# Attention and two MLPs on one core: a 4 KB descriptor ring, a seventh fp32 work tile, and one shared pool of six staging tiles

## The chip, the cores and the metric

The program runs on one core of one Trainium2 chip. The metric is the device time of one execution in microseconds (us). The engines are called PE (TensorE; PEld is its weight load), DVE (VectorE), ACT (ScalarE), POOL (GpSimd) and SP (SyncE, which here only issues DMAs). POOL issues DMAs too.

## The reference

Three stages follow each other. Each is two matrix products with something elementwise between them.

```python
scores = z @ z.T / S                 # B=2, S=3008, d_qk=64
x = u * (relu(scores) ** 2 @ v)      # d_model=256
h = x @ w_in                         # 6016 tokens, d_ff=2048
g = (a0 + a1*h + a2*h**2 + a3*h**3) / (1 + |b0|*|h| + |b1|*h**2 + 1e-6)
x = g @ w_out
h = x @ w2_in
out = (max(h, 0) + alpha * min(h, 0)) @ w2_out
```

The scores of one batch are symmetric, so a block above the diagonal is the transpose of one below it.

## The kernel before, in words

Products are kept near fp32 accuracy by splitting every operand into a high and a low part (`split`: ACT or DVE copies the high part, DVE subtracts at L121), so each product is three matmuls. Attention (`a_stream`) runs over blocks (b, j) of 512 query columns, six to a batch, and in a block over 12 steps kp of 256 key rows. A step makes two score tiles on PE (L393, L394), takes relu and square on ACT (L397, L400) into an fp32 tile `r`, splits it into `ahi` and `alo`, and three steps later (`LAG_A`) multiplies them with the values (L437, L446): 16 matmuls in all. The first MLP (`m1_hidden`, `m1_back`) is woven in between from step 36 of attention on, and weights are decoded, split and spilled to DRAM by POOL's DMAs meanwhile. The second MLP (`m2_*`) comes after attention, with the rest of the first.

For batch 1 (`FOLD`) the symmetry is used. In block j, every step whose key rows belong to a later block is also turned: `turn_block` lets SP issue two DMA transposes (L333) that read `r` as 16-bit words and write the staging tile `xt`, and `save_turned` stores `xt` to DRAM (`rt`, two DMAs at L341), one turn later. In the later block, `load_turned` brings the words back into a staging tile `xd` (two DMAs at L351), and `a_turned` joins them to fp32 (`rr`: ACT copies at L362, DVE at L363) in place of score matmuls. There are 30 turned steps, so 60 transposes, 60 stores and 60 loads.

All fp32 work tiles of 4 KB per partition (`r`, `rr`, `sq`, `ab`, `t`, `dec`, `m`) come from one tag `"t"` with TT = 6 buffers. An `r` that is turned holds its buffer until both its transposes have landed. `xt` has two buffers of its own (XT), and `xd` two (XD). Each engine and each DMA queue works strictly in order. The order on each is made by a scheduler when the program is built, which also chooses the buffer of each tile; a tile waits until the one before it in its buffer has been read for the last time. POOL's DMAs keep their descriptors in a ring at the start of SBUF, 16 KB per partition unless it is set otherwise.

Of the kernel before, what the change touches and what calls it, by code (L numbers as in the profile page):

```python
# [11 lines left out]
U16 = mybir.dt.uint16  # L12
# [3 lines left out]
DRAM = bass.MemoryType.DRAM  # L16


BIG, HL, TT, RAW, ZP, XP = 24, 7, 6, 2, 8, 4

XT, XD, AHEAD = 2, 2, 1

FOLD = ((1, 0),)

# [28 lines left out]
def relu2_attention_rational_mlp_prelu_mlp(  # L53
# [15 lines left out]
    nc = tc.nc  # L69
    P = 128  # L70
# [6 lines left out]
    QB = 512  # L77
# [18 lines left out]
    zctx = ExitStack()  # L96
    zp = zctx.enter_context(tc.tile_pool(name="zp", bufs=ZP))
    wr = zctx.enter_context(tc.tile_pool(name="wr", bufs=WR))
    xdp = zctx.enter_context(tc.tile_pool(name="xdp", bufs=XD))
    late = {}  # L100

    def raw_tile(nm, early=False):
# [173 lines left out]
    xd = {}  # L276
# [46 lines left out]
    def turn_block(b, j, kp, r):  # L323

        kb, k0 = kp // 2, kp % 2 * 2 * P
        if (b, j, kb) not in turned:
            turned[b, j, kb] = dr.tile([2, QB, QB], U16, name=f"rt{b}_{j}_{kb}")
        x = xdp.tile([P, 8, 2 * P], U16, tag="xt", name="xt", bufs=XT)
        ru = r.bitcast(U16)
        w = 0  # L330
        for i in range(2):
            rows = min(P, S - (2 * kp + i) * P)
            nc.sync.dma_start_transpose(out=x[:, :, w : w + rows], in_=ru[0:rows, i, :])  # L333
            w += rows
        unsaved.append((turned[b, j, kb], k0, w, x))
# [10 lines left out]
    def load_turned(b, j, kp):  # L346
        n = qn[j]
        q0 = kp % 2 * 2 * P
        d = xdp.tile([P, 2, 2, QB], U16, tag="xd", name="xd", bufs=XD)
        for h in range(2):  # L350
            nc.sync.dma_start(  # L351
                out=d[:, h, :, :n],
                in_=turned[b, kp // 2, j][h, q0 : q0 + 2 * P, :n].rearrange("(c p) k -> p c k", p=P),
            )
        halves[b, j, kp] = d
# [13 lines left out]
    def a_scores(b, j, kp):  # L369
# [43 lines left out]
        if folded(b, j, kp // 2):  # L413
            turn_block(b, j, kp, r)
# [255 lines left out]
    def a_stream():  # L670
# [4 lines left out]
        def fetch(b, j, kp):  # L675
            while coming and len(halves) < AHEAD + folded(b, kp // 2, j) and (
                coming[0][:2] == (b, j) or coming[0][:2] == (b, j + 1) and kp >= NKP - 2
            ):
                load_turned(*coming.pop(0))
# [190 lines left out]
```

## Time and profile before

| what | value |
|---|---|
| median of 3 runs | 1600.2 us (1598.0 to 1601.96) |
| the profiled execution: its own time | 1600.62 us |
| its span, first to last instruction | 1598.7 us |
| PE busy | 1539.4 us, 96% of the span |
| DVE, ACT, POOL busy | 1413.9, 1172.8, 90.5 us |
| mean granted clock of PE | 0.987 of full speed |

The page cuts the span in 40 slices of 40 us, with the busy tenths of each engine and the granted clock. All is full from slice 20 on, when attention has ended. Slices 9 to 19 are batch 1 of attention, where steps are turned and loaded back, and there PE and its clock show lower digits:

```profile
PE   9999999998989889888999999999999999999999
DVE  8989989896979788999999998999989899998864
PEclk9999999998999899999999999999999999999999
DMA  6364132569897878676700010100001000001000
```

PE and DVE are in tenths of a slice busy, PEclk in tenths of full clock, DMA the mean share of 16 DMA engines.

### The profile page before, as it was taken

How to read it: one execution, taken by the hardware profiler on the slowest of the kernel's cores; microseconds unless marked ns; L12 is line 12 of the kernel's file. 1: busy time of each engine (PE TensorE's matmuls, PEld its weight loads, DVE VectorE, ACT ScalarE, POOL GpSimd, SP SyncE). 2: the span in 40 equal slices, each digit the busy share in tenths (PEclk: the TensorE clock that was granted, in tenths of full speed). 3: DMA queues.
4: the chain of work that ended last, by engine and by line, in shares of the span. 5: the costliest groups of instructions: out<-in, count | busy, mean ns of one | idle time of the engine just before them, and what ended most of it. 6: DMA issues, size and time to landing. Idle time of an engine off the chain costs nothing.

```text
span 1598.7 us, 18271 instructions
## 1 busy us (share of the span) xinstructions
PE 1539.4 (96%) x6776; PEld 1271.4 (80%) x6776; DVE 1413.9 (88%) x1524; ACT 1172.8 (73%) x1405; POOL 90.5 (6%) x159
## 2 busy tenths in 40 slices
PE   9999999998989889888999999999999999999999
PEld 7887888786768667667788888888888888888888
DVE  8989989896979788999999998999989899998864
ACT  8989988897877878777676676667667676666644
POOL 1021000000001001101200000000000000000000
PEclk9999999998999899999999999999999999999999
DMA  6364132569897878676700010100001000001000
GB/s 203 101 208 148 59 106 73 163 148 228 235 210 209 175 221 157 192 197 214 259 2 27 27 40 1 40 12 28 27 27 40 1 27 28 35 1 40 14 1 23
DMA packets 155784, 157.76 MB, mean 99 GB/s; under 512 B 74016, under 2 KB 124720, under 8 KB 155696
## 3 DMA queue, kind: packets, MB, share of 16 engines
q1 hardware_dynamic: 134928, 93.67, 21.8%
q0 software_dynamic: 20768, 62.94, 13.4%
q8 instruction: 53, 0.87, 0.2%
q14 instruction: 35, 0.29, 0.1%
HBM read 92.94 MB, written 45.74 MB: 87 GB/s over the span
## 4 chain that ended last, share of the span: by engine, by line
PE 67%; DVE 11%; issue 9%; DMA 5%; ACT 5%; POOL 1%; SPq 0%; POOLq 0%; DVEq 0%; ACTq 0%
PE acc L437 18%; PE h L417 9%; PE h L419 9%; PE h L418 9%; PE acc L446 9%; PE acca L437 6%; PE acca L446 3%; DVE alo L121 2%; DMA wd<-dec 1%; PE s L393 1%; PE s L394 1%; DMA xt<-r 1%; PE acce L427 1%; DVE t L577 1%; ACT ahi L118 1%
## 5 line engine op out<-in xcount | busy, mean ns | idle before, releaser
L437 PE MATMUL acc<-ghi,w 128*128 128x512 f32 (+1 forms) x1472 | 365.9, 387 | 1.7 <-DVE ghi L575 1.7
L437 PEld LDWEIGHTS acc<-ghi,w 128*128 128x128 f32 x1472 | 275.3, 188 | 57.3 <-DVE ghi L575 1.6
L437 PE MATMUL acca<-ahi,vt 128*128 128x512 f32 (+1 forms) x1152 | 294.8, 394 | 10.5 <-ACT ahi L118 6.9
L417 PE MATMUL h<-xhi,w 128*128 128x512 f32 (+1 forms) x768 | 295.8, 386 | 4.1 <-DVE t L568 2.1
L418 PE MATMUL h<-xlo,w 128*128 128x512 f32 (+1 forms) x768 | 295.7, 385 | 1.1 <-DVE xlo L121 1.1
L419 PE MATMUL h<-xhi,w 128*128 128x512 f32 (+1 forms) x768 | 295.7, 385 | 0.0
L437 PEld LDWEIGHTS acca<-ahi,vt 128*128 128x128 f32 x1152 | 220.2, 192 | 58.4 <-ACT ahi L118 10.5
L446 PE MATMUL acc<-glo,w 128*128 128x512 f32 (+1 forms) x736 | 199.9, 390 | 10.5 <-DVE glo L578 10.3
L621 ACT ACTIVATE m<-h,sal 128x512 f32<-128x512 f32 (+1 forms) x192 | 127.4, 681 | 111.3 <-PE h L419 109.9
L561 ACT ACTIVATE sq<-h 128x1024 f32<-128x1024 f32 (+1 forms) x96 | 97.1, 1011 | 149.7 <-PE h L419 141.0
L417 PEld LDWEIGHTS h<-xhi,w 128*128 128x128 f32 x768 | 144.1, 188 | 35.4 <-issue 4.1
L446 PEld LDWEIGHTS acc<-glo,w 128*128 128x128 f32 x736 | 137.5, 188 | 41.9 <-DVE glo L578 14.9
L418 PEld LDWEIGHTS h<-xlo,w 128*128 128x128 f32 x768 | 144.1, 188 | 29.4 <-DVE xlo L121 1.9
L419 PEld LDWEIGHTS h<-xhi,w 128*128 128x128 f32 x768 | 144.1, 188 | 27.6
L121 DVE TENSOR_TENSOR glo<-m,ghi 128x1024 fp32r<-128x1024 f32 (+1 forms) x96 | 115.2, 1200 | 55.2 <-PE acc L437 42.0
L622 DVE SCALAR_TENSOR_TENSOR m<-h,sg,m 128x512 f32<-128x512 f32 (+1 forms) x192 | 138.1, 735 | 16.8 <-ACT m L621 15.3
L446 PE MATMUL acca<-alo,vt 128*128 128x512 f32 (+1 forms) x552 | 149.9, 389 | 0.0
L121 DVE TENSOR_TENSOR alo<-r,ahi 128x1024 fp32r<-128x1024 f32 (+2 forms) x103 | 122.9, 1195 | 17.9 <-PE acc L437 8.0
L397 ACT ACTIVATE r<-s 128x512 f32<-128x512 f32 (+1 forms) x184 | 104.2, 595 | 42.5 <-DMA xt<-r 24.3
L575 DVE SCALAR_TENSOR_TENSOR ghi<-t,sc,sq 128x1024 fp32r<-128x1024 f32 (+1 forms) x96 | 120.8, 1258 | 13.1 <-ACT sq L571 7.1
L565 DVE SCALAR_TENSOR_TENSOR ab<-sq,cb,ab 128x1024 f32<-128x1024 f32 (+1 forms) x96 | 120.8, 1258 | 9.9 <-ACT ab L562 9.7
L577 DVE SCALAR_TENSOR_TENSOR t<-t,sc,ab 128x1024 f32<-128x1024 f32 (+1 forms) x96 | 120.9, 1260 | 1.8
(96 smaller groups left out, 2222.8 us busy)
## 6 DMA issues: line engine op xcount, KB each, us to landing
w<-wd POOLq DMA_DIRECT2D x64, 512.0 KB, 4.9
rt<-xt SPq DMA_DIRECT2D x50, 256.0 KB, 3.1
wd<-dec POOLq DMA_DIRECT2D x48, 256.0 KB, 4.2
xd<-rt SPq DMA_DIRECT2D x40, 256.0 KB, 3.6
wraw<-in_moe_w_in_dram POOLq DMA_DIRECT2D x16, 512.0 KB, 4.3
wraw<-in_moe_w_out_dram POOLq DMA_DIRECT2D x16, 512.0 KB, 4.5
x2d<-x SPq DMA_DIRECT2D x11, 512.0 KB, 2.9
xr<-x2d SPq DMA_DIRECT2D x11, 512.0 KB, 3.3
```

The costliest lines, as they stand in the source:

```text
L121: nc.vector.tensor_tensor(dst_lo, src, dst_hi.bitcast(F32), ALU.subtract)
L397: nc.scalar.activation(r[:, i, :n], s, AF.Relu, scale=1.0 / S)
L417: nc.tensor.matmul(acc, w_hi, hi, start=first, stop=False)
L418: nc.tensor.matmul(acc, w_hi, lo, start=False, stop=False)
L419: nc.tensor.matmul(acc, w_lo, hi, start=False, stop=last)
L437: nc.tensor.matmul(acc[:, e, :n], w[:, k, i, e * P : (e + 1) * P], hi[i], start=first and i == 0 and k == 0, stop=False,)
L446: nc.tensor.matmul(acc[:, e, :n], w[:, 0, i, e * P : (e + 1) * P], lo[i], start=False, stop=last and i == both - 1,)
L565: nc.vector.scalar_tensor_tensor(ab, sq, b1, ab, ALU.mult, ALU.add)
L575: nc.vector.scalar_tensor_tensor(hi, t, a0, sq, ALU.add, ALU.mult)
L577: nc.vector.scalar_tensor_tensor(t, t, a0, ab, ALU.add, ALU.subtract)
L621: nc.scalar.activation(t[:, i], h, AF.Copy, scale=sal[:, f : f + 1])
L622: nc.vector.scalar_tensor_tensor(t[:, i], h, sg[:, f : f + 1], t[:, i], ALU.mult, ALU.max)
```

## The change

The ring of POOL's DMAs is set to 4 KB per partition. The 12 KB that come free hold one more buffer of the tag `"t"` (TT 6 to 7) and two more staging tiles. The staging tiles are no longer two of one kind and two of the other: `xt` and `xd` draw from one tag of six.

```diff
-BIG, HL, TT, RAW, ZP, XP = 24, 7, 6, 2, 8, 4
-XT, XD, AHEAD = 2, 2, 1
+BIG, HL, TT, RAW, ZP, XP = 24, 7, 7, 2, 8, 4
+XX, AHEAD = 6, 1
+RING = 4096
...
-    xdp = zctx.enter_context(tc.tile_pool(name="xdp", bufs=XD))
+    xdp = zctx.enter_context(tc.tile_pool(name="xdp", bufs=XX))
...
-        x = xdp.tile([P, 8, 2 * P], U16, tag="xt", name="xt", bufs=XT)
+        x = xdp.tile([P, 8, 2 * P], U16, tag="xx", name="xt")
...
-        d = xdp.tile([P, 2, 2, QB], U16, tag="xd", name="xd", bufs=XD)
+        d = xdp.tile([P, 2, 2, QB], U16, tag="xx", name="xd")
...
-    nc = _bacc.Bacc("TRN2", target_bir_lowering=False, num_devices=1)
+    nc = _bacc.Bacc("TRN2", target_bir_lowering=False, num_devices=1, dynamic_dma_scratch_size=RING)
```

No instruction is added or taken out. But with other buffers the scheduler orders the engines anew from the first MLP's start on, and gives other tiles the same buffer. In the changed file all lines from the tables on stand two further down.

The first place is SP's queue in block j = 0 of batch 1, in the middle of its turned steps. A name ends in the number of its tile, so `r_3245` and `xt_3259` belong to one step; `rt1_0_2` holds block (0, 2) turned, and `xd_3461` is a load for the next block. Before:

```order
L341 DMA rt1_0_2_3185<-xt_3186 64x8x256 x2
L351 DMA xd_3461<-rt1_0_1_3069 128x2x512 x2
L351 DMA xd_3583<-rt1_0_1_3069 128x2x512
L333 DMA_TRANSPOSE xt_3259<-r_3245 128x8x128 x2
L333 DMA_TRANSPOSE xt_3291<-r_3276 128x8x128 x2
L341 DMA rt1_0_2_3185<-xt_3259 64x8x256 x2
L341 DMA rt1_0_3_3290<-xt_3291 64x8x256 x2
L333 DMA_TRANSPOSE xt_3322<-r_3308 128x8x128 x2
```

Now:

```order
L343 DMA rt1_0_2_3185<-xt_3186 64x8x256 x2
L335 DMA_TRANSPOSE xt_3259<-r_3245 128x8x128 x2
L335 DMA_TRANSPOSE xt_3291<-r_3276 128x8x128 x2
L343 DMA rt1_0_2_3185<-xt_3259 64x8x256 x2
L335 DMA_TRANSPOSE xt_3322<-r_3308 128x8x128 x2
L343 DMA rt1_0_3_3290<-xt_3291 64x8x256 x2
L343 DMA rt1_0_3_3290<-xt_3322 64x8x256 x2
```

The loads have left this place, and the third pair of transposes stands ahead of the stores of the second.

The second place is SP's queue at the end of the same block, where its last turned step is `r_3548`. Before:

```order
L333 DMA_TRANSPOSE xt_3479<-r_3464 128x8x128 x2
L341 DMA rt1_0_4_3395<-xt_3444 64x8x256 x2
L341 DMA rt1_0_5_3478<-xt_3479 64x8x256 x2
L333 DMA_TRANSPOSE xt_3563<-r_3548 128x8x128
L333 DMA_TRANSPOSE xt_3563<-r_3548 128x8x64
L351 DMA xd_4086<-rt1_0_2_3185 128x2x512 x2
```

Now:

```order
L343 DMA rt1_0_4_3395<-xt_3444 64x8x256 x2
L343 DMA rt1_0_5_3478<-xt_3479 64x8x256 x2
L335 DMA_TRANSPOSE xt_3563<-r_3548 128x8x128
L335 DMA_TRANSPOSE xt_3563<-r_3548 128x8x64
L353 DMA xd_3583<-rt1_0_1_3069 128x2x512 x2
L294 DMA zB_4210<-zA_2649 64x512
```

The load of `xd_3583`, which stood in two halves 15 and 9 rows ahead of these transposes, now stands right behind them. `xd_4768` moves in the same way behind the last transposes of block j = 2.

The third place is ACT, at the same time. Before:

```order
L397 ACTIVATE r_3548<-s_3553 128x512
L571 ACTIVATE sq_3519<-sq_3519 128x1024
L400 ACTIVATE r_3548<-r_3548 128x1024
L362 COPY rr_3586<-xd_3461 128x1024
L362 COPY rr_3607<-xd_3583 128x1024
L407 CAST ahi_3558<-r_3548 128x1024
```

Now:

```order
L399 ACTIVATE r_3548<-s_3553 128x512
L573 ACTIVATE sq_3519<-sq_3519 128x1024
L402 ACTIVATE r_3548<-r_3548 128x1024
L364 COPY rr_3586<-xd_3461 128x1024
L409 CAST ahi_3558<-r_3548 128x1024
L364 COPY rr_3607<-xd_3583 128x1024
```

`rr_3607`, the reader of `xd_3583`, moved behind one instruction. It comes three instructions after the square of `r_3548`, for which the transposes ahead of its load wait.

## Rows read from the trace of the kernel before

**Rows 1.** Windows: stretch, then busy us (instructions) by engine, granted clock, DMA share, GB/s.
```profile
360.00:560.00 200.00, 178.86 (x747) 143.94 (x747) 163.65 (x173) 155.46 (x188) 17.57 (x29) 0.93 0.90 211
560.00:800.00 240.00, 214.02 (x908) 170.82 (x907) 217.16 (x229) 177.94 (x197) 28.30 (x50) 0.98 0.73 206
800.00:1400.00 600.00, 599.88 (x2644) 495.33 (x2644) 555.24 (x538) 402.04 (x462) 0.00 (x0) 1.00 0.07 24
```

**Rows 2.** Timeline of PE: start us, us, what, [idle before, who ended it].
```profile
389.45 0.80 PE L393 MATMUL s<-zA 128*128 128x512 f32 x1 [7.38 <-ACT r L397]
...
472.33 0.79 PE L393 MATMUL s<-zA 128*128 128x512 f32 x1 [5.56 <-ACT r L397]
...
548.82 0.80 PE L393 MATMUL s<-zA 128*128 128x512 f32 x1 [6.64 <-ACT r L397]
...
747.37 0.80 PE L446 MATMUL acc<-glo,w 128*128 128x512 f32 x1 [4.84 <-DVE glo L578]
```

**Rows 3.** Windows over the stretches of half clock behind those four waits.
```profile
384.20:394.40 10.20, 4.95 (x12) 3.93 (x13) 6.92 (x9) 5.30 (x9) 0.00 (x0) 0.50 0.93 200
469.60:476.30 6.70, 3.97 (x9) 3.14 (x10) 1.62 (x3) 4.50 (x6) 0.00 (x0) 0.50 1.12 254
544.70:554.80 10.10, 5.98 (x14) 4.73 (x15) 4.45 (x6) 6.63 (x9) 0.00 (x0) 0.50 0.70 174
746.10:752.80 6.70, 5.43 (x14) 4.84 (x15) 6.46 (x7) 5.39 (x6) 0.00 (x0) 0.50 0.44 137
```

**Rows 4.** Timeline of ACT at the first three of them.
```profile
388.80 1.09 ACT L397 ACTIVATE r<-s 128x512 f32<-128x512 f32 x2 [8.69 <-DMA xt<-r]
...
471.68 0.60 ACT L397 ACTIVATE r<-s 128x512 f32<-128x512 f32 x1 [5.75 <-DMA xt<-r]
...
548.17 1.08 ACT L397 ACTIVATE r<-s 128x512 f32<-128x512 f32 x2 [7.54 <-DMA xt<-r]
```

**Rows 5.** Chain that ended last, 360 to 480 us: start us, us, what.
```profile
376.34 7.40 DMA rt<-xt
383.82 1.30 SPq L333
385.16 3.53 DMA xt<-r
...
464.24 7.33 DMA xt<-r
```

**Rows 6.** Timeline of DVE at the first wait and at the fourth.
```profile
381.89 0.43 DVE L169 TENSOR_SCALAR dec<-wraw 128x512 f32<-128x512 f32 x1 [4.39 <-DMA xt<-r]
...
745.54 0.67 DVE L363 COPY rr<-xd 128x896 uint16<-128x896 uint16 x1 [3.38 <-DMA xd<-rt]
```

**Rows 7.** Timeline of SP's queue: transposes issued ahead of the second and third wait.
```profile
454.18 2.74 SPq L333 DMA_TRANSPOSE xt<-r  x2
...
526.00 7.94 SPq L333 DMA_TRANSPOSE xt<-r  x4
```

**Rows 8.** Waits of SP's queue, 360 to 800 us: total us, times, longest.
```profile
SPq L351 <- DVE rr L363: 75.2, 22, 7.7
```

**Rows 9.** Landing: transposes (view of L333); loads (page, part 6: KB, median us).
```profile
DMA to landing us min/median/max: 3.1/4.5/9.4
...
w<-wd POOLq DMA_DIRECT2D x64, 512.0 KB, 4.9
...
xd<-rt SPq DMA_DIRECT2D x40, 256.0 KB, 3.6
```

**Rows 10.** Timeline of ACT at the end of blocks j = 0 and j = 2.
```profile
408.39 2.59 ACT L362 COPY rr<-xd 128x1024 uint16<-128x1024 uint16 x2 [0.46 <-issue]
...
414.84 1.03 ACT L561 ACTIVATE sq<-h 128x1024 f32<-128x1024 f32 x1 [2.94 <-DVE t L577]
...
564.28 1.36 ACT L362 COPY rr<-xd 128x1024 uint16<-128x1024 uint16 x1 [4.44 <-DMA xt<-r]
```

**Rows 11.** Timeline of POOL's queue at the end of attention.
```profile
782.17 4.24 POOL L774 DMA_DIRECT2D w<-wd  x8 [0.31 <-DVE ut L482]
```

## The prediction

> **What bounds the kernel now.** I read the windows first, to find the stretch that has something to give. From 800 to 1400 us PE is busy 599.88 of 600 us at full clock [rows 1]: no buffer helps there. Batch 1 of attention, 360 to 800, is different: PE is busy 178.86 of 200 and 214.02 of 240 us, 392.9 of 440 us together, and its granted clock is below 1 [rows 1]. So 47.1 us of idle PE and some half-clock time are all that this change can reach.
>
> Next the timeline of PE, for the long waits. Four stand out: 7.38, 5.56 and 6.64 us before a score matmul that waits for ACT's `r`, and 4.84 us before a value matmul that waits for DVE [rows 2]. Behind each, PE's clock is 0.50, so 1.2 GHz in place of 2.4, for 6.7 to 10.2 us [rows 3]. PE had stood still just before each fall.
>
> Then who is behind ACT. At the first three, ACT stood still 8.69, 5.75 and 7.54 us and was released by a transpose that landed [rows 4]. This is a wait for a buffer: the new `r` may not be written until the old `r` in its buffer has been read by both transposes. The chain of waits tells why they were late. At the first, a store that SP issued at 376.34 took 7.40 us to land; only then, at 383.82, could the next transposes take its `xt` buffer, and their second half, issued at 385.16, landed 3.53 us later, at 388.69 [rows 5]. At the second, the last transpose was issued at 464.24 and needed 7.33 us [rows 5]. So both resources that the change adds are named in the waits: an `xt` buffer that SP lacks, and a `t` buffer that ACT lacks.
>
> The fourth wait is a load: DVE waits 3.38 us for `xd` [rows 6]. SP's queue shows the cause: between 360 and 800 us it stood 75.2 us, 22 times, with a load at its head until DVE had copied the tile two loads back [rows 8].
>
> **The change part by part.** No instruction is added, so all cost or gain is waits.
>
> *The seventh `t` buffer.* From the tile addresses of both built programs I read whose buffer each late `r` takes. At the first wait it is `r_3430`: before it follows `r_3308`, whose transposes landed at 388.69; now it follows `r_3276`, one turned step earlier. When that one's transposes landed is seen on DVE: `dec` had that buffer before, and DVE waited for them until 381.8 [rows 6]. ACT was free at 380.1 (388.80 − 8.69), so 1.7 us of 8.69 are left, less if the three loads that SP issues ahead of these transposes are gone from there, as the order shows. At the second it is `r_4089`, which now follows the `r` whose transposes SP had issued by 456.92 (454.18 + 2.74) [rows 7]; with the slowest landing of all, 9.4 us [rows 9], they are in at 466.3, when ACT has just run out of work (471.68 − 5.75 = 465.9). At the third it is `r_4655`, now behind a step whose transposes were issued by 533.94 [rows 7] and in by 538.4 at the median of 4.5, by 543.3 at the slowest [rows 9]; ACT ran out at 540.6 (548.17 − 7.54). So each of the three keeps about 0 to 2 us; I take 1.
>
> PE's three waits are 19.58 us. The half clock behind them costs half of what PE was busy then, as work at 1.2 GHz takes twice as long: (4.95 + 3.97 + 5.98) / 2 = 7.45 us. I add the clock only over PE's busy time since its idle time in those stretches is already in the waits. Together 27.0.
>
> *The shared pool of six.* Transposes no longer wait for the store before last, and loads no longer wait for the copy two loads back, so the 75.2 us at SP's head go; no engine waits for SP as such, only the fourth PE wait hangs on it. It is worth 4.84 + 5.43 / 2 = 7.56 us, and I leave 1 us of it. Could a long-held `xd` now block a turn? By the buffers, every `xt` that follows an `xd` stands 30 or more ACT instructions behind its last reader, so I price that at nothing; the cover is that distance.
>
> *Loads that moved.* `xd_3583` now stands behind the last transposes of block 0. From the square of `r_3548` on, SP needs 2.74 us for two transposes [rows 7], and ACT's half of the load lands 3.6 us after its issue [rows 9], so 6.3 us pass. ACT has two instructions of its own meanwhile, each 1.3 at most (a copy takes 2.59 / 2 [rows 10]). That leaves a new ACT wait of 3.7 us. Bounds: 0, if PE lives on its three-step lag, and 6.2 (3.7 and 2.5 of half clock, the mean of the four above). ACT stood still 2.94 us just behind this place anyway [rows 10], so I take 3.7 − 2.9 = 0.8. `xd_4768` does the same at block 2, but there ACT already lost 4.44 us to a transpose [rows 10], which goes; I price it at nothing, with the same upper bound.
>
> *The smaller ring.* POOL issued eight loads in a row in 4.24 us [rows 11], so the 16 KB ring held them. No row shows a full ring; the price lies between 0 and the case that POOL waits for each landing, 4.9 us [rows 9], 7 × 4.9 − 4.24 = 30 us later for the last weights. I take 0, as the eight share the same transfers whenever they are issued, and POOL is idle 94% of the span.
> The Trainium skill (DMA: Bandwidth & Descriptors, "SWDGE vs HWDGE vs iDMA") has descriptors of 16 bytes in rings on 16 partitions. An estimate from that page is 4096 / 16 = 256 for each of 16 DMA engines; a load of 128 rows puts 8 there and one for its semaphore, the eight loads 72. By it the price is 0 as well.
>
> **The sum.** 27.0 + 7.6 = 34.6, less 4 × 1 left over and 0.8 new: 29.8 us. A second limit checks this. DVE is busy 163.65 + 217.16 = 380.8 us between 360 and 800, and where PE never waits DVE runs at 555.24 / 600 = 92.5% [rows 1]. At that share the stretch takes 411.7 us, 28.3 less than now. The smaller of the two holds: DVE becomes the next to be late. Against the profiled execution (1600.62) that is **1572.3 us**; the median is only 0.4 lower, and I leave that.
>
> **Rivals.**
> *A. The wait moves one step on.* The transposes still land late (up to 9.4 us, where the quickest takes 3.1 [rows 9]), and the next `r` waits instead. Each wait then shrinks by the PE time of one step, 16 matmuls × 0.227 (599.88 / 2644 [rows 1]) = 3.6 us, three times 10.9; the clock still falls. With 7.6 from the loads and 0.8 to pay: 17.7 saved, 1582.9. For it: DMA share 0.90 in 360 to 560 [rows 1]. Against: the buffers above skip a whole turned step.
> The Trainium skill speaks for A (DMA: Bandwidth & Descriptors, "Rules for kernel authors"): DMAs issued from any engine run on the same 16 DMA engines. By it, buffers buy no transfer rate, and the time would be that of A. The trace agrees in part: the landings spread as far as those of a shared resource.
> *B. Slower: loads behind transposes.* In the new order 16 of the 30 loads stand within 17 ACT instructions of the square that the last transposes ahead of them wait for; before it was 8. A wait there costs up to 6.2 us. If PE outlives none of the eight new ones, five eat what the buffers bring (34.6 − 4 = 30.6), and with seven the time is 43.4 − 30.6 = 12.8 us up, 1613.4. Against: PE works three steps behind the scores, 3 × 12 × 0.227 = 8.2 us of value matmuls, more than one wait of 3.7.
> *C. The ring is too small.* Up to 30 us later weights at the end: 1602.5.
> *D. Nothing.* The scheduler's new order gives back what the buffers bring: about 1599.
>
> **How the numbers follow.** Forecast 0.54, A 0.28, D 0.06, B 0.05, C 0.03, better than forecast 0.04. Low end: 34.6 without leftovers or new waits, and a third of the other 22.7 us of idle PE (47.1 − 24.4): 42.2, so 1558. High end: A, with the moved load at its full 6.2: 1588.3; 1592 leaves a margin for a second one. Outside stay D, B and C, and a little below. About 0.3% (4.8 us) is what a measurement of this kernel can tell from no change. Faster by more: 0.54 + 0.27 of A + 0.04 = 0.85; within it 0.08 (D, and one in a hundred each of A and C); slower 0.07 (B and most of C).
>
> **What would show it.** Right: no wait of ACT's `r` for a transpose over 2 us, PE busy over 95% with clock near 1 from 360 to 560, the loads' 75 us at SP's head near 0, and a new ACT wait for `xd` of 2 to 4 us at the end of block 0. A: waits of 2 to 4 us for transposes, at other steps, each with half clock behind it. B: PE waits at each block's end. C: POOL's eight issues spread over 30 us. I am wrong if PE's half-clock time stays above 20 us (those four alone are 33.7 [rows 3]), or if something outside 360 to 800 moves by over 3 us.

## The result, and the profile after

The changed kernel takes **1577.62 us** (median of 3 runs, 1576.76 to 1583.07) where the kernel before took 1600.2: 0.987 of its time, with a 95% interval of 0.983 to 0.991. The profiled execution took 1577.62 us too, and its span is 1575.9. The forecast was 1572.3, the range 1558 to 1592. The sum came out 5 us off, but the time went elsewhere than the prediction said.

The slices of the page, where slices 9 to 19 were the thin ones:

```profile
PE   9999999999898989899999999999999999999999
...
DVE  8989989997898989999999998898989899898964
...
PEclk9999999999998989999999999999999999999999
DMA  6365222569796959677601010100101001001000
```

Of slices 15 to 19, three showed an 8 before (16 to 18), and one does now (16). In 9 to 14, where the prediction saw the most to gain, PE and its clock still dip. The windows that answer to [rows 1] say the same (stretch, busy us of PE, PEld, DVE, ACT, POOL, then clock, DMA share, GB/s):

```profile
360.00:560.00 200.00, 182.33 (x770) 148.02 (x769) 168.41 (x178) 156.34 (x189) 17.59 (x30) 0.94 0.90 221
560.00:800.00 240.00, 225.37 (x961) 181.04 (x960) 229.15 (x240) 185.72 (x207) 28.27 (x49) 0.98 0.66 191
800.00:1400.00 600.00, 600.00 (x2646) 496.06 (x2645) 553.54 (x537) 403.53 (x465) 0.00 (x0) 1.00 0.07 24
```

Such windows hold other work in a faster kernel. So I cut both runs where DVE multiplies the last block of a part by `u`: the end of batch 0, of block 2 of batch 1, and of attention. The two kernels then execute nearly the same number of PE instructions in a part. Before:

```profile
0.00:340.10 340.10, 331.65 (x1449) 272.69 (x1450) 310.18 (x402) 302.91 (x389) 42.09 (x76) 0.99 0.42 131
340.10:575.10 235.00, 211.48 (x886) 169.75 (x885) 193.11 (x202) 182.49 (x219) 20.68 (x34) 0.94 0.91 213
575.10:781.10 206.00, 185.73 (x790) 149.59 (x791) 188.21 (x203) 159.01 (x178) 22.99 (x40) 0.98 0.69 191
```

After:

```profile
0.00:335.00 335.00, 330.31 (x1450) 271.45 (x1451) 310.36 (x403) 302.89 (x389) 42.17 (x76) 1.00 0.43 133
335.00:564.20 229.20, 209.95 (x886) 169.95 (x884) 196.37 (x206) 184.81 (x222) 20.17 (x34) 0.95 0.91 222
564.20:757.80 193.60, 182.91 (x785) 148.57 (x786) 183.66 (x198) 155.71 (x175) 24.01 (x41) 0.97 0.70 199
```

The lengths give the ledger of the 22.8 us by which the span is shorter: 5.1 before batch 1, 5.8 in blocks 0 to 2, 12.4 in blocks 3 to 5, and 0.5 lost behind attention. Blocks 0 to 2 hold three of the four waits that the prediction counted, and gave 5.8 of the 23.2 us foreseen for them.

Two of the experiments below repeat the two orders. e1 has the order of the kernel before on every engine, and e6 has that of the changed kernel from batch 1 on. Their blocks 0 to 2, e1 first:

```profile
340.80:572.10 231.30, 211.70 (x886) 170.08 (x885) 193.04 (x202) 182.57 (x219) 20.75 (x34) 0.96 0.91 216
```

e6:

```profile
338.00:571.90 233.90, 211.15 (x885) 170.21 (x884) 196.38 (x205) 184.68 (x221) 20.16 (x34) 0.94 0.92 218
```

So this part takes 235.0 and 231.3 us in the old order, 229.2 and 233.9 in the new: the 5.8 us are within the spread of two profiles, and no gain is shown there. The 12.4 us in blocks 3 to 5 are shown (206.0 and 206.9 before, 193.6 and 194.4 after).

Where did those go? The three waits for `r` [rows 2] are gone, and three new ones stand nearly where they stood. Timeline of PE after:

```profile
399.07 0.80 PE L448 MATMUL acca<-alo,vt 128*128 128x512 f32 x1 [4.86 <-DVE alo L123]
...
488.53 0.79 PE L439 MATMUL acca<-ahi,vt 128*128 128x512 f32 x1 [7.78 <-ACT ahi L120]
...
557.08 1.22 PE L439 MATMUL acca<-ahi,vt 128*128 128x512 f32 x2 [4.55 <-ACT ahi L409]
```

PE now waits before value matmuls, at the ends of blocks 0, 1 and 2. As before, the granted clock is at 1.2 of 2.4 GHz behind each wait. The windows over these stretches answer to [rows 3]:

```profile
397.70:404.50 6.80, 5.43 (x13) 4.27 (x14) 6.49 (x7) 0.00 (x0) 0.00 (x0) 0.50 0.92 224
483.10:493.20 10.10, 4.67 (x11) 3.70 (x12) 4.43 (x6) 7.86 (x8) 0.55 (x1) 0.50 0.90 307
554.80:561.50 6.70, 4.42 (x10) 3.47 (x11) 4.71 (x6) 6.70 (x7) 0.00 (x0) 0.50 1.03 319
```

By the prediction's own way of counting, these three cost 4.86 + 7.78 + 4.55 = 17.2 us of idle PE and (5.43 + 4.67 + 4.42) / 2 = 7.3 of half clock: 24.5, where the three waits for `r` had cost 27.0. Behind each of them stands a load, no longer a transpose. In each, the matmul needs a split part (`ahi` or `alo`) of an earlier step, and this split stands behind the copy of the late load in the order of DVE or ACT. At the first it is DVE, which stood for `xd_3461`; `alo` of `r_3464` comes two instructions behind that copy. Timeline of DVE:

```profile
396.04 0.74 DVE L365 COPY rr<-xd 128x1024 uint16<-128x1024 uint16 x1 [8.01 <-DMA xd<-rt]
...
397.79 1.22 DVE L123 TENSOR_TENSOR alo<-r,ahi 128x1024 fp32r<-128x1024 f32 x1
```

At the other two it is ACT, which stood for `xd_4241` and `xd_4768`:

```profile
485.34 1.33 ACT L364 COPY rr<-xd 128x1024 uint16<-128x1024 uint16 x1 [7.44 <-DMA xd<-rt]
...
554.79 1.33 ACT L364 COPY rr<-xd 128x1024 uint16<-128x1024 uint16 x1 [8.89 <-DMA xd<-rt]
```

`xd_3461` is one of the loads that left SP's queue in the middle of the turned steps. SP issued it 19 us later than before, and its halves landed at 394.89 and 395.82. Timeline of SP before (the third of these is half of `xd_3583`):

```profile
366.81 1.83 SPq L351 DMA_DIRECT2D xd<-rt  x3
```

After:

```profile
385.84 2.15 SPq L353 DMA_DIRECT2D xd<-rt  x2
```

The load that the prediction priced, `xd_3583`, held up ACT for 8.04 us, but not PE, which had no wait of over 0.5 us from 400 to 414:

```profile
405.23 1.37 ACT L364 COPY rr<-xd 128x1024 uint16<-128x1024 uint16 x1 [8.04 <-DMA xd<-rt]
```

The waits of ACT and DVE, from 330 to 800 us (us in total, times, longest), show who stood. Before:

```profile
ACT r L397 <- DMA xt<-r: 24.3, 5, 8.7
...
ACT rr L362 <- DMA xd<-rt: 7.0, 3, 3.6
...
ACT rr L362 <- DMA xt<-r: 4.4, 1, 4.4
DVE dec L169 <- DMA xt<-r: 4.4, 1, 4.4
...
DVE rr L363 <- DMA xd<-rt: 3.4, 1, 3.4
...
DVE rr L363 <- DMA xt<-r: 2.3, 1, 2.3
```

After:

```profile
ACT rr L364 <- DMA xd<-rt: 32.0, 6, 8.9
...
DVE rr L365 <- DMA xd<-rt: 14.5, 3, 8.0
```

ACT and DVE together stood 35.4 us for transposes and 10.4 for loads before; now it is 0.4 and 46.5. **The sum is 45.8 before and 46.9 after.** By part it is 34.0 before and 40.0 after in blocks 0 to 2, 11.9 and 6.9 in blocks 3 to 5. Both engines can stand at once, so this is not time lost. But in blocks 0 to 2 the buffers changed who waits and did not make the waits less.

SP's head wait for a copy two loads back [rows 8] did fall, from 75.2 to 12.7 us:

```profile
SPq L353 <- DVE rr L365: 12.7, 2, 8.2
```

The chain of waits shows how the load of `xd_3583` came to be late (start us, us, what):

```profile
392.11 5.58 DMA xt<-r
...
397.76 0.58 SPq L343
...
398.39 0.64 SPq L343
...
399.12 1.40 SPq L335
...
400.56 1.47 SPq L335
...
402.07 3.06 DMA xd<-rt
```

The load stands where the order said, behind the last two transposes (L335). But ahead of those come stores (L343), and two of them had to wait until the transposes of `r_3464` landed, 5.58 us after the second was issued. The square of `r_3548` was done at 392.2; the load was issued at 402.07.

### The profile page after: what moved, and what is told of

Read it like the earlier page. It is cut to its first block, busy times and chain, and to the rows that moved or that the text cites. A ratio compares the mean times of both kernels' runs of the same rounds, so it can differ in the third digit from the quotient of the medians.

```text
span 1575.9 us, 18162 instructions
## 1 busy us (share of the span) xinstructions
PE 1535.3 (97%) x6776; PEld 1270.2 (81%) x6776; DVE 1413.7 (90%) x1524; ACT 1172.7 (74%) x1405; POOL 90.6 (6%) x159
## 4 chain that ended last, share of the span: by engine, by line
PE 75%; DVE 7%; ACT 6%; issue 5%; DMA 5%; SPq 1%; POOL 1%; DVEq 0%; ACTq 0%; POOLq 0%
PE acc L439 19%; PE h L419 10%; PE h L420 10%; PE h L421 10%; PE acc L448 9%; PE acca L439 8%; PE acca L448 4%; PE s L395 2%; PE s L396 2%; DVE alo L123 1%; DMA wd<-dec 1%; DMA xt<-r 1%; DMA xd<-rt 1%; PE acce L429 1%; ACT ahi L120 1%
## 5 line engine op out<-in xcount | busy, mean ns | idle before, releaser
L448 PEld LDWEIGHTS acca<-alo,vt 128*128 128x128 f32 x552 | 104.7, 190 | 26.1 <-DVE alo L123 6.0
```

Source lines behind the costliest of these rows:

```text
L448: nc.tensor.matmul(acc[:, e, :n], w[:, 0, i, e * P : (e + 1) * P], lo[i], start=False, stop=last and i == both - 1,)
```

## The experiments

Each has one profiled execution and a median over several runs, with its ratio to the kernel before on the same chip. **Lost time** is PE's idle time and half of what it was busy at half clock. A part is cut as above.

| kernel | median us | ratio, 95% | to end of batch 0 | blocks 0-2 | blocks 3-5 | lost in 0-2 | waits for xt + xd |
|---|---|---|---|---|---|---|---|
| before | 1600.2 | | 340.1 | 235.0 | 206.0 | 31.0 | 35.4 + 10.4 |
| after | 1577.6 | 0.987 (0.983-0.991) | 335.0 | 229.2 | 193.6 | 26.6 | 0.4 + 46.5 |
| e1 ring | 1600.2 | 1.001 (0.999-1.003) | 340.8 | 231.3 | 206.9 | 27.6 | 30.3 + 18.9 |
| e2 seventh tile | 1579.7 | 0.987 (0.985-0.990) | 334.8 | 224.5 | 202.6 | 22.0 | 26.8 + 28.0 |
| e3 pool | 1593.9 | 0.997 (0.995-0.999) | 339.2 | 233.7 | 201.4 | 30.2 | 32.0 + 24.4 |
| e4 split 2 + 4 | 1578.7 | 0.986 (0.983-0.988) | 335.8 | 233.1 | 191.3 | 28.3 | 51.0 + 0 |
| e5 nine tiles | 1584.5 | 0.992 (0.990-0.993) | 335.9 | 226.9 | 200.3 | 24.1 | 7.1 + 38.2 |
| e6 extra DMA, too early | 1582.0 | 0.989 (0.985-0.994) | 338.0 | 233.9 | 194.4 | 30.9 | 6.0 + 47.5 |
| e7 spills moved | 1584.4 | 0.992 (0.989-0.994) | 340.0 | 216.3 | 203.9 | 14.3 | 0 + 33.0 |
| e8 block 0 not turned | **1553.4** | 0.972 (0.971-0.974) | 334.8 | 208.6 | 193.1 | 2.8 | 6.8 + 3.5 |
| e9 e8 with busy DMA | 1564.9 | 0.978 (0.976-0.980) | 336.1 | 219.4 | 190.0 | 13.4 | 13.0 + 2.9 |
| e10 before, block 0 not turned | 1582.0 | 0.988 (0.985-0.990) | 341.7 | 218.4 | 203.1 | 10.6 | 14.3 + 12.7 |
| e11 block 0 partly turned | 1565.0 | 0.978 (0.975-0.980) | 335.9 | 211.2 | 197.1 | 4.4 | 4.0 + 7.6 |
| e12 e4, block 0 not turned | 1561.5 | 0.976 (0.972-0.979) | 335.4 | 217.4 | 190.0 | 10.0 | 9.9 + 0 |

Profiles of one order (before and e1, after and e6) differ by up to 4.7 us in blocks 0 to 2 and 4.3 in the time lost there. Smaller differences between rows say nothing.

The first theory was that the late loads of the shared pool had eaten some 25 us, and that loads standing early would bring them back. Four runs take the change apart.

**e1, the ring alone.**

```diff
-    nc = _bacc.Bacc("TRN2", target_bir_lowering=False, num_devices=1)
+    nc = _bacc.Bacc("TRN2", target_bir_lowering=False, num_devices=1, dynamic_dma_scratch_size=4096)
```

> The kernel before with the 4 KB ring alone; every engine has the same instructions in the same order and every tile the same number of buffers. Theory (the ring costs nothing, all gain is buffers): 1600 us, within 3 us of the kernel before, and the eight weight loads near 782 us are still issued in some 4 us. Rival C (a ring of 4 KB fills and POOL waits for landings): 1605 to 1630, the eight issues spread over 10 to 30 us. Rival E (the ring's size itself moves something at the start, such as the 4 us that the changed kernel gained near 300 us): 1594 to 1597.

No change, to within 0.3%. The stall near 300 us is still there (4.34 us). The ring is free here.

**e2, ring and seventh tile** (against the kernel before, as e3 to e5; the ring's line is not repeated).

```diff
-BIG, HL, TT, RAW, ZP, XP = 24, 7, 6, 2, 8, 4
+BIG, HL, TT, RAW, ZP, XP = 24, 7, 7, 2, 8, 4
```

> The kernel before with the 4 KB ring and the seventh work tile alone; two xt and two xd tiles of their own, as before. The loads of turned halves stay early: the two at the end of block 0 stand 50 and 35 ACT instructions behind the last transposes ahead of them on SP, where the shared pool has 17 and 3. Theory (the seventh tile cures the waits of r, and the late loads of the shared pool cost some 25 us of what the change had to give): the three waits of 5 to 8 us before score matmuls go (27 us with their clock), no wait for a loaded half above 4 us comes at the ends of blocks 0 to 2, the wait of 4.8 us near 745 stays: 1568 to 1577, so no slower than the changed kernel. Rival F (the stores still hold up the transposes with two xt tiles, so a wait of r moves one step on): waits of 3 to 5 us for transposes remain at three places, 1583 to 1590. Rival G (the shared pool does it all): 1597 to 1602.

The same total as the whole change, so the seventh tile alone is worth as much, though 2.7 us above the theory's range. It comes from other parts: blocks 0 to 2 take 224.5 us and blocks 3 to 5 202.6, against 229.2 and 193.6. And the theory's reason falls: these loads stand early, and ACT and DVE still stood 28.0 us for loads, the longest 8.2. They stood 26.8 for transposes, 22.4 of it with `rr`, which comes from the same tag as `r`.

**e3, ring and shared pool** (the change with TT left at 6; the three lines of the staging tiles are as there).

```diff
-XT, XD, AHEAD = 2, 2, 1
+XX, AHEAD = 6, 1
...
```

> The changed kernel with six work tiles in place of seven: the ring and the shared pool of six alone. The loads stand as late as in the changed kernel. Theory (the pool cures the waits at SP's head and the wait near 745, but its late loads cost some 25 us, and with six tiles r still waits for transposes): 1595 to 1612, with waits of ACT and DVE for loaded halves of 20 us or more in sum, as in the changed kernel, and waits of r for transposes beside them. Rival G (the pool lets transposes go earlier, and that alone cures r's waits): 1573 to 1583.

A small gain, 0.3%, close under the range, in the profile mostly in blocks 3 to 5 (206.0 to 201.4); waits for transposes and loads side by side, as the theory said. Rival G is out.

**e4, seven tiles, two `xt` and four `xd`.**

```diff
-BIG, HL, TT, RAW, ZP, XP = 24, 7, 6, 2, 8, 4
+BIG, HL, TT, RAW, ZP, XP = 24, 7, 7, 2, 8, 4
...
-XT, XD, AHEAD = 2, 2, 1
+XT, XD, AHEAD = 2, 4, 1
```

> The 4 KB ring, seven work tiles, and the six staging tiles not shared: two xt, four xd. Each load stands at least 14 ACT instructions behind the last transposes ahead of it, where the shared pool has 2 and 3 at the ends of blocks 2 and 0. Theory (late loads are what the shared pool costs): the waits of ACT and DVE for loaded halves, 46 us in sum between 360 and 800 with the shared pool, fall below 10; PE's waits of 4.9, 7.8 and 4.6 us near 394, 481 and 552 go, and the one near 745 stays gone: 1555 to 1566. Rival H (DVE is the limit at 92.5% busy, so what is taken from one wait comes back as another): 1571 to 1578, PE waiting for DVE in many places of 1 to 3 us. Rival F (two xt tiles hold up the transposes): waits of r for transposes of 3 to 6 us, 1575 to 1590.

This run fells the theory. Every load is in time: the waits for them are 0. The time is that of the change all the same, since `r`, `rr` and others of the same tag now wait for a buffer whose transposes have not landed. Waits of e4, 330 to 800 us:

```profile
DVE rr L363 <- DMA xt<-r: 15.8, 3, 9.9
ACT r L397 <- DMA xt<-r: 15.4, 3, 6.5
...
ACT rr L362 <- DMA xt<-r: 12.7, 4, 5.8
...
DVE dec L169 <- DMA xt<-r: 4.9, 1, 4.9
...
ACT ab L562 <- DMA xt<-r: 2.2, 1, 2.2
```

PE's longest wait, 9.48 us at 410, is for DVE, which stood 9.93 for such a buffer; so it is not DVE's own work, as rival H had it. Rival F held, for the waits and the time: loads put first make transposes late, transposes put first make loads late. In five arrangements of buffers (before, after, e2, e3, e4) the two sums of the last column add up to 45.8, 46.9, 54.8, 56.4 and 51.0 (in the repeats e1 and e6 to 49.2 and 53.5). That gave the second theory, M: in blocks 0 to 2, where the DMA share is 0.90 to 0.98, the load on the DMA engines sets the time.

**e5, nine tiles.**

```diff
-BIG, HL, TT, RAW, ZP, XP = 24, 7, 6, 2, 8, 4
+BIG, HL, TT, RAW, ZP, XP = 24, 7, 9, 2, 8, 4
```

> The 4 KB ring with all 12 KB put into work tiles: nine in place of six, two xt and two xd as before. PE's lost time (idle, and half of what it was busy at half clock) in blocks 0 to 2 of batch 1 was 31 us in the kernel before, 27 in the changed kernel, 22 with the seventh tile alone, 28 with two xt and four xd. Theory M (in these blocks the DMA engines, busy 90 to 98%, are the limit, and buffers and order only choose who waits): lost 20 to 28 us there, 1574 to 1582. Rival N (work tiles are still too few, each r holds one until its transposes land): lost below 14 there, 1560 to 1569.

Rival N is out: 24.1 us stay lost in blocks 0 to 2, inside M's bounds, and the total is 2.5 us over them. One load alone holds PE up for 17.10 us (timeline of PE):

```profile
495.58 0.79 PE L437 MATMUL acca<-ahi,vt 128*128 128x512 f32 x1 [17.10 <-ACT ahi L118]
```

**e6, more DMA traffic in the changed kernel** (`now[0]` is the step).

```diff
+        if 72 <= now[0] < 108:
+            nc.gpsimd.dma_start(out=dr.tile([P, 2, 512], F32R, name=f"extra{now[0]}_{len(w1d)}_{jp}"), in_=w1d[id(store), jp])
         store[jp] = t
...
+        now[0] = st
```

> The changed kernel with more DMA traffic and nothing else: each weight reload that the program places in blocks 0 to 2 of batch 1 is followed on POOL's queue by a copy of the same 512 KB from DRAM to DRAM that nobody reads; all other instructions and their order stay. That is some 11 copies, 5.8 MB beside 44 MB. Theory M: the stretch needs over a tenth more of what is already 90% busy, so landings and PE's lost time in blocks 0 to 2 grow by 6 to 25 us: 1584 to 1603. Rival O (only SP's order of issue matters, the transfers have room): within 4 us of the changed kernel, 1574 to 1582.

1582.0 us (ratio 0.989, 0.985 to 0.994), and nothing follows for M: the copies depended on no late work, so the order put ten of them at 99 to 151 us, ahead of the blocks that they were meant for. From batch 1 on all engines have the order of the changed kernel, so this profile serves as its repeat. e9 puts the traffic where it was meant.

**e7, weight spills moved out of blocks 0 and 1.**

```diff
-SP, AV0, AV1 = 5, 64, 76
+SP, AV0, AV1 = 5, 71, 91
```

> The changed kernel with the decoding of the second MLP's weights kept out of steps 71 to 90, where blocks 0 and 1 of batch 1 are: four of the 16 are moved (two before, the rest behind). Each takes 0.5 MB in and 0.5 MB out of the DMA engines, so some 3 to 4 MB of 44 leave blocks 0 to 2, and about 3 DVE instruction groups of 4 us with them. Theory M: PE's lost time in blocks 0 to 2 falls from 27 to 12 to 20 us, some of it comes back in blocks 3 to 5 where DVE is 95% busy: 1566 to 1575. Rival O (SP's order alone): lost time as in the changed kernel, 1575 to 1582.

Half right. Lost time in blocks 0 to 2 fell to 14.3, as M said. But the decoding is work for DVE and for the `t` tiles, too, and came back where it went: 5.0 us more before batch 1, 10.3 more in blocks 3 to 5 than in the changed kernel. The total is worse, outside M's range. As DVE's work moved along, the run can't tell DMA from DVE.

**e8, block 0 of batch 1 not turned.**

```diff
-FOLD = ((1, 0),)
+FOLD = ((1, 1),)
```

> The changed kernel with block 0 of batch 1 not turned: 20 of 60 transposes, stores and loads go, and ten steps of later blocks make their scores by four matmuls each, 40 x 0.227 = 9 us more on PE. Theory M: DMA share in blocks 0 to 2 falls below 0.75 and PE's lost time there from 27 to 8 to 16 us; with the 9 us more: 1570 to 1580. Rival O' (what is lost in blocks 0 to 2 has nothing to do with the transfers, but with DVE and ACT): lost time there as now, and the 9 us on top: 1584 to 1592.

Faster than M dared: 24 us below the changed kernel, although PE has 40 more score matmuls to do. Lost time in blocks 0 to 2 is 2.8 us, and the waits for transposes and loads are 10.3 us together. The parts (blocks 0 to 2, 3 to 5):

```profile
334.80:543.40 208.60, 205.83 (x896) 166.53 (x895) 190.16 (x198) 187.08 (x231) 19.88 (x34) 1.00 0.70 174
543.40:736.50 193.10, 186.62 (x816) 153.49 (x815) 183.67 (x196) 159.14 (x184) 23.82 (x41) 0.98 0.69 195
```

DMA share went from 0.91 to 0.70, the clock to 1.00. This kernel beats both others. But SP's queue and DVE's work were relieved along with the DMA engines. The next run parts them.

**e9, e8 with busy DMA engines.** Only POOL's queue differs from e8; PE, ACT, DVE and SP do the same in the same order.

```diff
         store[jp] = t
+        if last and 91 <= now[0] < 112:
+            for c in range(3):
+                d = dr.tile([P, 2, 2, 256], F32R, name=f"extra{len(last)}_{c}")
+                nc.gpsimd.dma_start(out=d, in_=last[-1])
+        last.append(t)
...
+        now[0] = st
```

> The kernel with block 0 of batch 1 not turned (1553 us, PE's lost time in blocks 0 to 2 2.8 us), with more DMA traffic in blocks 1 and 2 and nothing else: some 18 copies of 512 KB from a weight tile to DRAM, on POOL's queue and chained to the weight loads so that they run between 400 and 540 us; every other engine and SP's queue have the same instructions in the same order. Theory M (the load on the DMA engines makes the turned steps late): DMA share goes to about 1 from 400 to 540, transposes land later, and PE's lost time in blocks 0 to 2 grows to 10 to 30 us: 1560 to 1585. Rival O (fewer turned steps help because SP's queue holds fewer of them): lost time below 6 us, 1551 to 1558.

18 copies ran from 408 to 513 us, and M holds: ratio 0.978 in place of 0.972, 9 us, and blocks 0 to 2 longer by 10.8. Both from 460 to 500 us, e8 first:

```profile
460.00:500.00 40.00, 37.24 (x162) 29.72 (x161) 36.88 (x44) 32.91 (x41) 5.24 (x9) 1.00 0.83 229
```

e9:

```profile
460.00:500.00 40.00, 31.64 (x128) 25.33 (x127) 26.22 (x30) 23.38 (x28) 7.84 (x15) 0.87 1.16 313
```

The waits that come are the known ones. ACT's timeline in e9:

```profile
475.74 1.09 ACT L399 ACTIVATE r<-s 128x512 f32<-128x512 f32 x2 [6.97 <-DMA xt<-r]
...
482.33 1.33 ACT L364 COPY rr<-xd 128x1024 uint16<-128x1024 uint16 x1 [5.50 <-DMA xt<-r]
```

The share rose from 0.83 to 1.16 and PE did 5.6 us less; it loses 8.36 us behind those two waits. With buffers, order and every other engine's work the same, DMA traffic alone makes turned steps late. The copies did not act through the weights: ACT's waits for spills in blocks 0 to 2 are 4.9 us in e8 and 3.8 here. How much of the 26.6 us lost in the changed kernel is this load, and how much is SP's order, no run tells.

**e10, the kernel before with block 0 not turned** (the diff of e8, on the kernel before).

> The kernel before (16 KB ring, six work tiles, two xt and two xd) with block 0 of batch 1 not turned: none of the change. Theory M (the waits of r were the same overload, and buffers help little once it is gone): PE's lost time in blocks 0 to 2 below 10 us, 10 before batch 1 and some 15 to 20 in blocks 3 to 5 as before: 1563 to 1573. Rival P (the seventh tile and the pool are worth as much as with block 0 turned): 1574 to 1581.

Rival P is nearer, and M's second half falls: buffers are not worthless once the load is gone. The change is worth 0.972 / 0.988, 1.6%, on top of e10, about what it is worth alone. Each part gives some: 6.9 us before batch 1, 9.8 in blocks 0 to 2, 10.0 behind.

**e11, four of block 0's ten steps turned** (against e8).

```diff
-        return i < j and any(b == fb and i >= f0 for fb, f0 in FOLD)
+        return i < j and any(b == fb and (i >= f0 or j >= 4) for fb, f0 in FOLD)
```

> The changed kernel with only the last four of the ten turned steps of block 0 turned (those for blocks 4 and 5), in place of none (1553 us) or ten (1578 us). Four steps less of score matmuls are 16 x 0.227 = 3.6 us less on PE. Theory M (DMA has room there, a share of 0.28 to 0.42 from 340 to 420 with none turned): lost time grows by less than 3 us, 1547 to 1553. Rival Q (any turned step in block 0 brings the late loads at its end back): lost time 10 us up or more, 1558 to 1568.

A miss, some 8.5 us above e8 by the ratios (0.978 and 0.972). Blocks 0 to 2 behave as M said (4.4 us lost), and rival Q's late loads don't come. The rest is in blocks 3 to 5, where 17.5 us are lost in place of 9.8, 4.76 of them in one gap near 601 us that the profile can put down to nothing. Why stays open.

**e12, e4's buffers with block 0 not turned.**

```diff
-FOLD = ((1, 0),)
+FOLD = ((1, 1),)
```

> The 4 KB ring, seven work tiles, two xt and four xd of their own, and block 0 of batch 1 not turned. With block 0 turned, this split and the shared pool gave the same time (1578.7 and 1577.6 us) with PE's lost time in blocks 3 to 5 at 12 and 15 us; with the shared pool and block 0 not turned it is 1553 us, 2.8 us lost in blocks 0 to 2 and 9.8 in blocks 3 to 5. Theory M (once the DMA engines have room, how the six staging tiles are shared matters little): 1549 to 1557, lost time within 4 us of the shared pool's in either part. Rival F (two xt tiles hold up the transposes by the stores): waits of r and of copies for transposes above 15 us in sum, 1560 to 1570.

Between the ranges: no sum of waits for transposes above 15 us, so not F, but 4.5 us above M's end. Blocks 0 to 2 lose 10.0 us, 7.2 more than in e8, where M allowed 4. The DMA share there is 0.70 in both, so buffers and order count at this load, as in e10. The interval of the total touches that of e8, so whether the shared pool makes the faster program here is not settled.

## Why the prediction was right in the sum and wrong in the places

- **The seventh tile cures the three waits for `r`.** Right for `r`: 24.3 us of ACT's waits for transposes went to 0, which is better than the 1 us each that was left over. But with that tile alone (e2) `r` stands 4.4 us, and `rr`, from the same tag, 22.4.
- **The pool clears SP's head and the fourth wait.** Right: 75.2 to 12.7 us, and PE has no wait of over 2 us left between 675 and 800. Blocks 3 to 5 gave 12.4 us where 6.6 were foreseen. The seventh tile alone gives 3.4 there (e2) and the pool alone 4.6 (e3), so it takes both; the tile with two more `xd` gives 14.7 (e4).
- **The ring at 0.** Right (e1).
- **Loads that moved, priced at 0.8 and 0.** This is the term that failed. It measured 24.5 us, at three places: 7.6 for `xd_3461`, 10.1 for `xd_4241` and 6.8 for `xd_4768`. Of these the prediction had listed only `xd_4768`, at 0 with a bound of 6.2. `xd_3583`, which it took at 0.8, made ACT wait 8.0 us where 3.7 were foreseen, and made PE wait for nothing. Three readings were wrong. A load's landing was taken at the median of 3.6 us [rows 9]: `xd_3461` took 9.1 us (385.84 to 394.89) and `xd_4241` 7.5. SP's path from the square to the load of `xd_3583` was taken as two transposes, 2.74 us; it was 9.9, as the stores and the landings that they wait for were not counted. And the lag of 8.2 us of value matmuls, the case against rival B, does not help where the split of an earlier step stands behind the copy of the late load on its engine, as it does at all three places.
- **Rival A** had the better mechanism for blocks 0 to 2: the wait moved on, though to the loads and not to the next `r`. It leaned on the rule that DMAs from any engine run on the same 16 DMA engines (the Trainium skill, DMA: Bandwidth & Descriptors, "Rules for kernel authors"). e9 agrees with it: copies on POOL's queue brought 13.0 us of waits for SP's transposes, in place of 6.8. The time can't tell A from the forecast: it lies 5.3 us from either. **Rival B's** loads behind transposes came at block ends, as it said, but did not make the kernel slower.
- **The second limit, DVE at 92.5%.** It set the forecast, 28.3 us in place of the sum's 29.8. It fits blocks 3 to 5 only, where DVE is busy 183.66 of 193.6 us, 95%. In blocks 0 to 2 it is 196.37 of 229.2, 86%: there the limit was another.
- **Not foreseen:** 5.1 us before batch 1. At 294.6 us ACT's `ab` stood for a tile of tag `"t"`:

```profile
299.27 1.11 ACT L562 ACTIVATE ab<-h,cb 128x1024 f32<-128x1024 f32 x1 [4.68 <-DVE t L577]
```

That is the kernel before; PE waited 3.85 us behind it. Kernels with six such tiles all keep this stall (e1 4.34, e3 3.83, e10 4.30), the changed kernel, e2, e4 and e5 don't. The prediction asked only what the tile does for `r`, and took the idle and half-clock time from 360 to 800 us for all that the change can reach.

So 23.2 us foreseen in blocks 0 to 2 became 5.8, which the repeats do not confirm, and the 6.6 and 0 elsewhere became 12.4 and 5.1. From 360 to 560 us PE is busy 91% of the time at a clock of 0.94, where the prediction wanted over 95% near 1. Both signs that the prediction named as its failure came true: PE's half clock is 34.1 us long in all behind the waits (41.0 before), and a part outside 360 to 800 moved by over 3 us. The total was near because the errors offset each other, and that is luck.

## What to carry to other kernels

Add up all engines' waits for one stream of DMAs before pricing a buffer: where the DMA share is as high as here (0.90 and more), a buffer can pass the wait to another tile and leave the sum. A load that a new order puts behind other DMAs is to be priced by its landing in that crowded stretch, and by all that its queue must do first, stores and their own waits too. Then look at what stands behind its copy on the engine that copies: that waits with it. Repeat a profile before reading a difference of a few us in a part. And ask who else draws on the tag that gets a tile. What helped most was to send less: leaving ten steps unturned cost 40 matmuls and gave 24 us.

## What the hardware showed that was not expected

The DMA share is not capped at 1: e9 shows 1.16, and 313 GB/s, from 460 to 500 us, where blocks 0 to 2 of the kernel before have 0.91 and 213 GB/s. So the rate of those blocks is not the most that the engines move; what more load does is make single DMAs late (from 340 to 570 us transposes landed after 3.8 us at the median in e8, after 4.8 in e9). Nor need the share be near 1 on the mean to hurt. In e9 that of blocks 0 to 2 rose from 0.70 to 0.80, most of it from 408 to 513 us (1.02, in e8 0.86), and the part took 10.8 us more. Between 340 and 570 us the same 256 KB loads landed after 3.9 us at the median and 5.8 at most before, after 5.5 and 10.5 in the changed kernel, which has 24 of them in that stretch in place of 17, right among the stores and transposes.
